# Stores of kept weights, first gates and output transposes: moved in a fused attention, Mish and Sinkhorn-MoE kernel

## The chip, the cores and the metric

One NeuronCore of one Trainium2 chip. The metric is the device time of one execution in microseconds (us). Its engines work side by side, each through its own program in order: TensorE (PE; its weight loads are PEld), VectorE (DVE), ScalarE (ACT), GpSimd (POOL) and SyncE (SP). All DMAs of the part shown here are issued by SP, whose queue also is in order: a DMA that waits for a semaphore holds back those behind it. [...]

## The reference

Three parts in a row, in float32.

- A gated delta-rule attention: 4 batches, 8 heads, 768 positions, head size 48. Keys are normalized, and a 48x48 state per head runs over the positions: `y_t = q_t S`, then `S += beta_t k_t (v_t - k_t S)`.
- A Mish MLP on the 3072 tokens of width 384: `h = x @ w_in` (2048 wide), `g = h * tanh(softplus(h))`, `g @ w_out`.
- A mixture of 8 experts with Sinkhorn gates: `P = exp(logits)` of 3072x8, scaled eight times by row sums and by column sums, then `out = sum over e of P[:, e] * (relu(x @ w1[e]) @ w2[e])`, each expert 1024 wide.

## The kernel before, in words

Each float32 product is made of three products of rounded high and low parts (weights high and low by inputs high, weights high by inputs low), so every operand has a high tile, copied by ACT, and a low tile, a difference made by DVE or POOL.

**First stage.** Six windows (`c` = 0 to 5) of 512 tokens. A window runs 16 Mish units (marks s0 to s15), and then 8 units of expert 0 (marks s16 to s23), each unit with 128 hidden columns. Attention for the next windows is hung on the marks. Weights cycle through six slots (`wslots`): from the second window on each unit's split weights come back from a copy in DRAM by a DMA of 768 KB on SP's queue (line 251, `w<-wd`), issued some three units ahead.

In the last window the second stage is prepared at marks s1 to s15: raw weights of experts 1 to 7 come in (`fetch1` line 432, `fetch2` line 442), ACT and POOL split them (`make1`, `make2`) into three slots `gw`, and `keep` (line 445) stores each split slot to DRAM, `wg`, in two parts of 1280 and 768 KB: units 0 to 2 at marks s5, s6, s9, s10, s13 and s14. While the 8 units of expert 0 run, DVE works off the Sinkhorn rounds, and the gates `P` are final when that stage ends.

**Second stage.** Three units of tokens (`u`, 1024 tokens each), each with 28 steps (7 experts by 4 groups of 256 hidden columns), so 84 steps `s`. A step runs seven groups of first products (line 589, tile `b`, 3 or 6 matmuls each, in the order of `ORDER` = 0, 2, 1, 4, 3, 5, 6; a Strassen-like scheme of seven products). After each group `k` = 0 to 6 come, in this order on the queues: what drains the group into `gt` (DVE line 596, ACT line 598 for the first), the low parts that `late` holds, a weighing of a finished hidden block by its gate and the ReLU (`weigh`: DVE line 622, ACT line 628, low part line 631 on POOL in unit 0 and on DVE after), what `side[k]` holds, five of the 36 second products of the step before (line 652, into six PSUM banks `s`; the last group takes six), and perhaps one `o_store`. First products take their bank from a ring, two banks of `ps_a` as a rule, four in step 0.

In step 0 no second products are there. The weighings wait in `done` until the last group, and each is followed at once by its low part. The gate of expert 1 for the first tokens is spread over partitions in `gate_first`: one DVE multiply of an identity by the gate column (line 547, 128x1024), then two products with a matrix of ones at group 1 (line 555) that ACT copies out (line 556). `gate_out` writes all gates to DRAM: a DVE copy (line 527), two transposes (line 530), an ACT copy (line 532) and two DMAs at group 3; `gate_load` of expert 2 follows at group 4, the others come later, each two steps or more ahead of its use.

At a unit's end the second products of its last step run beside the next unit's first step. After product 26 of 36 half 0 is complete, after product 35 half 1. `o_out` then copies the three banks of a half to `gf` (ACT lines 675 twice, DVE line 673) and puts four stores on `todo`. `o_store` takes one: a bank of the ring, three transposes (line 688), a DVE multiply-add with the gate of expert 0 (line 689) and two output DMAs (line 695). In the loop one store is made after each odd group, so the first one directly behind the copies. Of the last unit no first products are left: its 36 second products run through, with half 0 complete after product 17, and the eight stores follow.

The right side of the on-chip memory is filled from its end: a tile `pad` of 32 bytes a partition, then the weight slots of the first stage and, in the second, `gt`, the high and low hidden tiles, one of the two `gx` tiles and the gates.

Of the kernel before, what the change touches and what calls it, by code (L numbers as in the profile page):

```python
# [8 lines left out]
F32 = mybir.dt.float32  # L9
# [3 lines left out]
AF = mybir.ActivationFunctionType  # L13
# [71 lines left out]
def delta_mish_sinkhorn_kernel(  # L85
# [18 lines left out]
    out_r = out.rearrange("(b s) d -> b s d", b=B)  # L104

    const = ctx.enter_context(tc.tile_pool(name="const", bufs=1))
    ctx.enter_context(tc.tile_pool(name="pad", bufs=1, side="right")).tile([128, 8], F32, name="pad")
    right = ExitStack()
    wpool = right.enter_context(tc.tile_pool(name="wpool", bufs=1, side="right"))
    rawp = ctx.enter_context(tc.tile_pool(name="rawp", bufs=2))  # L110
# [313 lines left out]
        pool2["q"] = ctx.enter_context(tc.tile_pool(name="gq", bufs=1, side="right"))  # L424

    raw1, raw2, wd2 = {}, {}, []

    def fetch1(n):
        if n < UPER:
# [13 lines left out]
            raw2[n] = r  # L443

    def keep(n, lo, hi):
        nc.sync.dma_start(out=wd2[n][:, :, lo:hi], in_=gslots[n % NS2][:, :, lo:hi].bitcast(F32))

    def again(n, lo, hi):
# [75 lines left out]
    def gate_out():  # L524

        q = pool2["q"].tile([128, 3, 192], F32, name="gq")
        nc.vector.tensor_copy(q[:, 0].rearrange("p (e t) -> p e t", e=E), P.rearrange("p t e -> p e t"))
        ps = small[0]()
        for a in range(2):
            nc.tensor.transpose(ps[0:96, a * 128:a * 128 + 128], q[:, 0, a * 96:a * 96 + 96], id_sb)  # L530
        rows = q[0:96, 1:3].rearrange("p a x -> p (a x)")[:, 0:256]
        nc.scalar.activation(out=rows, in_=ps[0:96, 0:256], func=AF.Copy)
        for a in range(2):
            nc.sync.dma_start(out=pe_dram[0][96 * a:96 * a + 96, :], in_=rows[:, 128 * a:128 * a + 128])

    def gate_load(u, e):
        pb = pool2["p"].tile([128, 1024], F32, tag="p", name="gp")
# [6 lines left out]
    def gate_first():  # L544

        a, pb = (pool2["p"].tile([128, 1024], F32, tag="p", name="gp") for _ in range(2))
        nc.vector.tensor_tensor(
            out=a.rearrange("p (t x) -> p t x", x=128), in0=id_sb[:, None, :].to_broadcast([128, 8, 128]),
            in1=P[:, 0:8, 1:2].to_broadcast([128, 8, 128]), op=ALU.mult,
        )  # L550

        def spread_out():
            for i in range(2):
                ps = next_ring("pb")
                mm(ps, lhsT=sk["ones"], rhs=a[:, 512 * i:512 * i + 512], start=True, stop=True)
                nc.scalar.activation(out=pb[:, 512 * i:512 * i + 512], in_=ps, func=AF.Copy)
            pbs[0, 1] = pb

        return spread_out

    ring, ringn = [], [0]

# [94 lines left out]
            seen.add(half)  # L657
        return out

    fin = {}  # L660

    def o_open(u):
        f = pool2[u % 2, "x"].tile([128, 6, 1024], F32, tag="x", name="gf")
# [5 lines left out]
    def o_out(u, half):  # L669
        for d in range(KD):  # L670
            o = fin[u][:, d, 512 * half:512 * half + 512]
            if d == 1:
                nc.vector.tensor_copy(o, os[u][3 * half + d])
            else:
                nc.scalar.activation(out=o, in_=os[u][3 * half + d], func=AF.Copy)
        for t in range(4):
            todo.append((u, half, t))

# [27 lines left out]
    if True:  # L706
# [756 lines left out]
        with tc.manual_schedule():  # L1463
            banks[:] = [0, [A1, A1]]
            for c in range(NBLK):
                pe, rest, late = window(c)
                if c == NBLK - 1:
                    p1.close()
                    open_second()
                    for n in range(2):  # L1470
                        rest["s1"].append(lambda n=n: (fetch1(n), fetch2(n)))
                    rest["s1"].append(lambda: x_fetch(0, 0))
                    for n, f in enumerate((5, 9, 13)):
                        rest[f"s{f}"].append(lambda n=n: all_of(make1(n)))
                        rest[f"s{f + 1}"].append(lambda n=n: all_of(make2(n)))
                    for q, at in enumerate(((3, 4, 7), (11, 12, 15))):
                        for k, f in enumerate(at):
                            if k == 0:
                                rest[f"s{f}"].append(lambda q=q: all_of(x_sums(0, q)))
                            rest[f"s{f}"].append(lambda q=q, k=k: x_split(0, q, k))  # L1480
                    rest["s8"].append(lambda: x_fetch(0, 1))
                m0 = PLACES[0][0]
                b = c * NU

                def side_pe(m, part):
                    return [st() for st in (pe[m][2:] + late[m] if part else pe[m][:2])]

                def side_rest(m, posts):
                    for p in posts:
                        p()  # L1490
                    for r in rest[m]:
                        r()
                    for p in side_pe(m, 1):
                        p()

                rate(0.6)
                for f in range(U1 + 3):
                    m = MARKS[f]
                    posts = side_pe(m, 0)
                    if f < U1:  # L1500
                        ready(b + f)
                        m_first(b + f)
                    if 1 <= f <= U1:
                        m_a(b + f - 1)
                        m_c(b + f - 1)
                    if f == 0 and c:
                        y0_second(b - 1)
                    if f == 1 and c:
                        y0_done(c - 1)
                    if f == 4:  # L1510
                        flush_xr()
                    if f == 2 or not c:
                        banks[1] = [A1, A1, (ps_o1, "o3")]
                    if f == U1 + 1:
                        m_second(b + U1 - 1)
                        x2_done(c)
                    side_rest(m, posts)
                    if 2 <= f <= U1:
                        m_second(b + f - 2)
                    fill(2.0 if c else 1.2)  # L1520
                    if f < U1:
                        if not c:
                            decodes(min(U1, f + 4))
                            converts(min(U1, f + 3))
                            begins(min(U1, f + 5))
                        if ncvt[0] >= U1:
                            conversions(b + f)
                side_rest("f4", side_pe("f4", 0))
                fill(2.0)
                banks[1] = [A1, A1]  # L1530
                last = c == NBLK - 1
                for f in range(U1, NU):
                    u = b + f
                    if last and f > U1 and f % 2 == 0:
                        sink_step()
                    posts = side_pe(f"s{f}", 0)
                    ready(u)
                    if f == U1 + 2:
                        flush_xr()
                    e_first(u, ps_h, mi_p, x1h, x1l)  # L1540
                    if f > U1:
                        e_relu(u - 1)
                    side_rest(f"s{f}", posts)
                    if f > U1:
                        fill(3.6 if c == 0 else 3.2)
                    if last and f > U1 and (f % 2 == 1 or f == U1 + 2):
                        sink_step()
                    if f > U1 + 1:
                        y0_second(u - 2, sink_step if last and f % 2 == 0 and f > U1 + 2 else None)
                    conversions(u)  # L1550
                e_relu(b + NU - 1)
                split = [lambda kc=kc: st_x1(c + 1, kc) for kc in range(KD)] if c + 1 < NBLK else []
                if split:
                    run(*split[0:2])
                y0_second(b + NU - 2)
                if split:
                    run(split[2])
# [9 lines left out]
    with tc.manual_schedule():  # L1567
# [5 lines left out]
        for s in range(N + 1):  # L1573
            ops = seconds(s - 1) if s else []
            if s == N:
                for n, one in enumerate(ops):
                    one()
                    if late and n == 0:
                        late.popleft()()
                while todo:  # L1580
                    o_store()
                break
# [1 line left out]
            k2 = s % UPER  # L1584
            side = {k: [] for k in range(7)}
            if s == 0:
                side[1].append(gate_first())
                side[3].append(gate_out)
                side[4].append(lambda: gate_load(0, 2))
            if s and s + 2 < UPER:  # L1590
                parts = make1(s + 2)
                for k, p in zip((2, 2, 3, 3, 5), parts):
# [27 lines left out]
            for k, a in enumerate(ORDER):  # L1620
                z = drain(s, a, first(s, a))
                while late:
                    late.popleft()()
                if s == 0:
                    done += [z] if z is not None else []
                elif z is not None:
                    late.append(weigh(s, z))
                for p in side[k]:
                    p()
                for one in ops[5 * k:5 * k + 5 if k < 6 else None]:  # L1630
                    one()
                if todo and k % 2 == 1:
                    o_store()
            for z in done:
                late.append(weigh(s, z))
                late.popleft()()
            if s == 0:
                ring[:] = [A1, A1]
                ringn[0] = 0
# [66 lines left out]
```

## Time and profile before

| | us |
|---|---|
| median of 3 runs | 2297.07 |
| the three runs | 2296.84, 2305.61, 2297.07 |
| the profiled execution | 2303.45 |
| its span, first to last instruction | 2301.7 |
| mean granted TensorE clock, share of full speed | 0.971 |

The profile is one execution, and its times are counted from its first instruction. The first stage ends at some 935 us, the second runs to the end. A group of instructions is named by its line, the tile written and the tile read. Of a wait the profile names the releaser that came last.

### The profile page before, as it was taken

The numbers are of one execution on the slowest core, as the hardware profiler recorded it, in microseconds if no ns is written. First come the engines' busy times: TensorE is split into PE (matmuls) and PEld (weight loads), VectorE is DVE, ScalarE is ACT, GpSimd is POOL, SyncE is SP. The second block draws the span as 40 slices with busy tenths as digits, with TensorE's granted clock in tenths as the row PEclk, the third lists the DMA queues.
The fourth block names the chain that finished last, engine by engine and source line by source line (L and its number), as shares of the span: only waits on it lengthen the run. The fifth ranks groups of instructions, "written<-read, shape, count | busy, mean of one in ns | idle before, by whom it ended". The sixth has DMA issues, their size and how long they took to land.

```text
span 2301.7 us, 34912 instructions
## 1 busy us (share of the span) xinstructions
PE 2221.2 (97%) x14262; PEld 1817.4 (79%) x14262; DVE 1356.0 (59%) x2214; ACT 648.2 (28%) x1148; POOL 620.8 (27%) x488
## 2 busy tenths in 40 slices
PE   8788899999999999999999999999999999999998
PEld 6667788788888887788888887888888878888886
DVE  7894726336162134767767766666666666566665
ACT  6453331433323243233333321112112121111111
POOL 4504441432402153376776850000000000000000
PEclk7699999999999999999999999999999999999999
DMA  6385734646354477255555555443443444434342
GB/s 179 128 291 178 238 125 142 183 149 209 128 177 149 162 281 260 75 185 190 195 207 193 190 174 181 151 155 132 157 153 119 176 147 155 139 136 156 124 141 69
DMA packets 121103, 384.25 MB, mean 167 GB/s; under 512 B 9968, under 2 KB 46768, under 8 KB 120944
## 3 DMA queue, kind: packets, MB, share of 16 engines
q1 hardware_dynamic: 120944, 382.03, 48.8%
q8 instruction: 112, 1.84, 0.3%
q14 instruction: 47, 0.39, 0.0%
HBM read 290.14 MB, written 91.85 MB: 166 GB/s over the span
## 4 chain that ended last, share of the span: by engine, by line
PE 87%; DVE 8%; issue 2%; POOL 1%; DMA 1%; ACT 1%; SPq 0%; DVEq 0%; POOLq 0%; ACTq 0%
PE s L652 30%; PE b L589 28%; PE psh L307 11%; PE x L1211 7%; PE y L331 4%; DVE t L993 1%; DVE lane L999 1%; PE psa L930 1%; PE psa L1069 1%; DMA w<-wd 1%; PE psa L1125 1%; PE psa L1230 1%; PE psa L1091 1%; PE psa L1035 1%; DVE lane L963 1%
## 5 line engine op out<-in xcount | busy, mean ns | idle before, releaser
L589 PE MATMUL b<-gx,gw 128*128 128x512 f32 x2772 | 733.9, 393 | 0.1
L596 DVE TENSOR_TENSOR gt<-b,gt 128x512 f32<-128x512 f32 x588 | 398.4, 690 | 423.0 <-PE b L589 412.4
L589 PEld LDWEIGHTS b<-gx,gw 128*128 128x128 f32 x2772 | 519.4, 188 | 116.4 <-DVE gt L596 1.4
L652 PE MATMUL s<-gh,gw 128*128 128x512 f32 x2016 | 575.0, 394 | 1.4 <-ACT gh L628 1.4
L628 ACT ACTIVATE gh<-gt 128x512 fp32r<-128x512 f32 x336 | 212.3, 632 | 968.6 <-DVE gt L622 968.6
L652 PEld LDWEIGHTS s<-gh,gw 128*128 128x128 f32 x2016 | 378.8, 188 | 89.4 <-ACT gh L628 1.8
L307 PE MATMUL psh<-xh,w 128*128 128x512 f32 x864 | 287.8, 415 | 18.9 <-DVE gl L1200 8.4
L652 PE MATMUL s<-gl,gw 128*128 128x512 f32 x1008 | 301.1, 393 | 0.0
L622 DVE SCALAR_TENSOR_TENSOR gt<-gt,gp 128x512 f32<-128x512 f32 x336 | 284.9, 849 | 4.7
L652 PEld LDWEIGHTS s<-gl,gw 128*128 128x128 f32 x1008 | 189.7, 188 | 43.1
L307 PEld LDWEIGHTS psh<-xh,w 128*128 128x128 f32 x864 | 159.6, 194 | 61.8 <-DVE gl L1200 12.4
L1200 POOL TENSOR_TENSOR gl<-x,gh 128x512 fp32r<-128x512 f32 x80 | 103.0, 1288 | 380.6 <-ACT gh L1198 367.5
L631 POOL TENSOR_TENSOR gl<-gt,gh 128x512 fp32r<-128x512 f32 x112 | 165.8, 1488 | 132.5 <-ACT gh L628 70.0
L307 PE MATMUL psh<-xl,w 128*128 128x512 f32 x432 | 175.4, 406 | 0.4 <-DVE xl L786 0.4
L631 DVE TENSOR_TENSOR gl<-gt,gh 128x512 fp32r<-128x512 f32 x224 | 153.2, 684 | 35.2 <-ACT gh L628 35.1
L1211 PE MATMUL x<-gh,w 128*128 128x512 f32 x576 | 153.4, 403 | 0.0
L522 POOL TENSOR_TENSOR gx<-gxr,gx 128x768 fp32r<-128x768 f32 x18 | 33.4, 1858 | 377.9 <-ACT gx L521 376.6
L1211 PEld LDWEIGHTS x<-gh,w 128*128 128x128 f32 x576 | 110.6, 194 | 24.2 <-issue 0.3
L453 POOL TENSOR_TENSOR gw<-gr,gw 128x640 fp32r<-128x640 f32 x56 | 93.3, 1668 | 50.2 <-ACT gw L463 50.2
L307 PEld LDWEIGHTS psh<-xl,w 128*128 128x128 f32 x432 | 84.3, 195 | 21.2 <-DVE xl L786 2.1
L331 PE MATMUL y<-w,hh 128*128 128x384 f32 x384 | 99.3, 339 | 0.0
L1192 ACT ACTIVATE x<-psh 128x512 f32<-128x512 f32 x80 | 47.8, 597 | 144.2 <-PE psh L307 139.8
(196 smaller groups left out, 2271.4 us busy)
## 6 DMA issues: line engine op xcount, KB each, us to landing
w<-wd SPq DMA_DIRECT2D x120, 768.0 KB, 4.4
gw<-wg SPq DMA_DIRECT2D x56, 1280.0 KB, 8.0
gw<-wg SPq DMA_DIRECT2D x56, 768.0 KB, 5.1
wg<-gw SPq DMA_DIRECT2D x28, 1280.0 KB, 6.0
wg<-gw SPq DMA_DIRECT2D x28, 768.0 KB, 5.4
wd<-w SPq DMA_DIRECT2D x24, 768.0 KB, 4.9
gr<-in_w_dram SPq DMA_DIRECT2D x28, 384.0 KB, 3.3
raw<-in_w_dram SPq DMA_DIRECT2D x28, 384.0 KB, 4.0
```

The costliest lines, as they stand in the source:

```text
L307: mm(ps, lhsT=wi(u, pw, kc), rhs=(xh, xl)[px][:, kc, :], start=(n == 0), stop=(n == 3 * KD - 1))
L331: mm(o[t], lhsT=(h, l)[ph][:, t * 128:(t + 1) * 128], rhs=wo(u, pw, 0, DM), start=(f == 0 and n == 0), stop=(f == U2 - 1 and n == 2))
L453: nc.gpsimd.tensor_tensor(out=w[:, 1, lo:hi], in0=r, in1=w[:, 0, lo:hi].bitcast(F32), op=ALU.subtract)
L589: mm(ps, lhsT=w[:, pw, i * 128:i * 128 + 128], rhs=x[:, px, j, :], start=(n == 0), stop=(n == last))
L596: add = lambda o, i: nc.vector.tensor_tensor(out=t[:, o], in0=ps, in1=t[:, i], op=ALU.add)
L622: nc.vector.scalar_tensor_tensor(out=t, in0=t, scalar=0.0, in1=pbs[u, e][:, o:o + 512], op0=ALU.max, op1=ALU.mult)
L628: nc.scalar.activation(out=h, in_=t, func=AF.Copy)
L631: return lambda: eng.tensor_tensor(out=l, in0=t, in1=h.bitcast(F32), op=ALU.subtract)
L652: mm(os[u][3 * half + d], lhsT=w[:, pw, at:at + 128], rhs=hids[s, z][ph], start=(start and new and n == 0), stop=(end and not new and n == 2))
L1192: nc.scalar.activation(out=mi_x[u % 2], in_=hps.pop(u), func=AF.Mish)
L1200: eng.tensor_tensor(out=l, in0=p, in1=h.bitcast(F32), op=ALU.subtract)
L1211: mm(x2ps[c][k], lhsT=wo(u, pw, k * 128, k * 128 + 128), rhs=(h, l)[pg], start=(f == 0 and n == 0), stop=(f == U1 - 1 and n == 2))
```

## The change

The pad grows from 32 to 96 bytes a partition. `keep` puts the stores of units 0 to 2 on a list, and one of the six is issued at each of the marks s17 to s22, beside expert 0. The first gates are made by eight ACT copies of 128x128 with the gate column as scale, and spread in two parts at groups 2 and 3; `gate_out`'s copy goes to ACT, behind group 4, and its transposes, DMAs and the load of expert 2's gate come behind group 6. In step 0 the weighings start at group 4, and their low parts come one group later. A unit's output stores start three groups after a half is complete and then come every second group. In the last products four stores are made between products (after 23, 26, 29 and 32), one at product 35, with three more banks in the ring.

```diff
-    ....tile([128, 8], F32, name="pad")
+    ....tile([128, 24], F32, name="pad")
...
     def keep(n, lo, hi):
+        if n < NS2:
+            kept.append(lambda: store(n, lo, hi))
+        else:
+            store(n, lo, hi)
+
+    def store(n, lo, hi):
         nc.sync.dma_start(out=wd2[n][:, :, lo:hi], in_=gslots[n % NS2][:, :, lo:hi].bitcast(F32))
...
     def gate_out():
-        nc.vector.tensor_copy(q[:, 0].rearrange(...), P.rearrange("p t e -> p e t"))
-        ps = small[0]()
+        nc.scalar.activation(out=q[:, 0].rearrange(...), in_=P.rearrange("p t e -> p e t"), func=AF.Copy)
+        def turn():
+            ps = small[0]()
...
+            gate_load(0, 2)
+        return turn
...
     def gate_first():
-        nc.vector.tensor_tensor(out=a..., in0=id_sb[:, None, :]..., in1=P[:, 0:8, 1:2]..., op=ALU.mult)
-        def spread_out():
-            for i in range(2):
-                ps = next_ring("pb")
-                mm(ps, lhsT=sk["ones"], rhs=a[:, 512 * i:512 * i + 512], start=True, stop=True)
-                nc.scalar.activation(out=pb[:, 512 * i:512 * i + 512], in_=ps, func=AF.Copy)
+        for t in range(8):
+            nc.scalar.activation(out=a[:, 128 * t:128 * t + 128], in_=id_sb, func=AF.Copy, scale=P[:, t, 1:2])
+        def spread_out(i):
+            ps = next_ring("pb")
+            mm(ps, lhsT=sk["ones"], rhs=a[:, 512 * i:512 * i + 512], start=True, stop=True)
+            nc.scalar.activation(out=pb[:, 512 * i:512 * i + 512], in_=ps, func=AF.Copy)
...
     def o_out(u, half):
+        slot[0] = 3
...
+                    for f in range(U1 + 1, NU - 1):
+                        rest[f"s{f}"].append(lambda: kept.popleft()())
...
             if s == N:
+                ring.extend((ps_o1, f"o{k}") for k in range(3))
                 for n, one in enumerate(ops):
                     one()
...
+                    if n > 22 and n % 3 == 2 and todo:
+                        o_store()
...
             if s == 0:
-                side[1].append(gate_first())
-                side[3].append(gate_out)
-                side[4].append(lambda: gate_load(0, 2))
+                spread_out = gate_first()
+                for i in range(2):
+                    side[2 + i].append(spread_out[i])
+                turn = []
+                side[4].append(lambda: turn.append(gate_out()))
+                side[6].append(lambda: turn[0]())
...
-                if s == 0:
-                    done += [z] if z is not None else []
-                elif z is not None:
-                    late.append(weigh(s, z))
+                if z is not None:
+                    done.append(z)
+                if s or k > 3:
+                    for z in done:
+                        late.append(weigh(s, z))
+                    done = []
...
-                if todo and k % 2 == 1:
+                slot[0] -= 1
+                if todo and slot[0] < 0:
                     o_store()
-            for z in done:
-                late.append(weigh(s, z))
-                late.popleft()()
+                    slot[0] = 1
```

## Rows read from the trace of the kernel before

**Rows 1.** The page, part 1: busy time of TensorE, its share, instructions.

```profile
PE 2221.2 (97%) x14262; PEld 1817.4 (79%) x14262; DVE 1356.0 (59%) x2214; ACT 648.2 (28%) x1148; POOL 620.8 (27%) x488
```

**Rows 2.** The page, part 2: clock granted to TensorE in 40 equal slices.

```profile
PEclk7699999999999999999999999999999999999999
```

**Rows 3.** Waits of PE, whole run: us in total, times, longest.

```profile
PE psh L307 <- DMA w<-wd: 5.2, 2, 3.0
PE of L688 <- ACT gf L675: 4.1, 2, 2.1
```

**Rows 4.** Timeline of PE at the end of the kernel.

```profile
2279.56 1.54 PE L652 MATMUL s<-gh,gw 128*128 128x512 f32 x6
2287.80 0.82 PE L688 MATMUL of<-id_sb,gf 128*128 128x128 f32 x6
```

**Rows 5.** Timeline of PE, last mish window: start, us, line, operation, [idle before <-releaser].

```profile
848.56 0.70 PE L307 MATMUL psh<-xh,w 128*128 128x512 f32 x2 [2.96 <-DMA w<-wd]
854.33 0.62 PE L307 MATMUL psh<-xh,w 128*128 128x512 f32 x2
869.01 0.69 PE L307 MATMUL psh<-xh,w 128*128 128x512 f32 x2 [2.28 <-DMA w<-wd]
879.29 0.62 PE L307 MATMUL psh<-xh,w 128*128 128x512 f32 x2
```

**Rows 6.** Stretch around the first stall: busy by engine, PEclk, DMA share, GB/s.

```profile
843.00:856.00 13.00, 10.04 (x38) 7.85 (x37) 0.00 (x0) 3.62 (x5) 4.38 (x4) 0.87 1.02 345
```

**Rows 7.** Chain of waits in the same window: start, us, what.

```profile
839.01 9.42 DMA w<-wd
860.16 8.71 DMA w<-wd
```

**Rows 8.** The page, part 6: issues, KB each, median us to landing.

```profile
w<-wd SPq DMA_DIRECT2D x120, 768.0 KB, 4.4
```

**Rows 9.** Timeline of SP's queue in the same window.

```profile
837.91 0.38 SPq L432 DMA_DIRECT2D gr<-in_w_dram  x1
```

**Rows 10.** DMA traffic from 835 to 870 us: packets, MB, share.

```profile
q1 hardware_dynamic: 3852, 10.23, 83.7%
```

**Rows 11.** DMA traffic from 890 to 935 us, in 40 slices.

```profile
GB/s 418 317 339 421 426 431 419 393 421 421 410 142 38 0 44 257 377 22 0 120 366 213 0 0 0 15 0 0 0 0 0 0 0 0 0 0 0 0 0 0
```

**Rows 12.** Timeline of PE at the first unit's end.

```profile
1389.57 1.54 PE L589 MATMUL b<-gx,gw 128*128 128x512 f32 x6
1394.35 0.82 PE L688 MATMUL of<-id_sb,gf 128*128 128x128 f32 x3 [2.10 <-ACT gf L675]
1399.36 0.85 PE L589 MATMUL b<-gx,gw 128*128 128x512 f32 x3
```

**Rows 13.** Timeline of DVE at the end of the kernel.

```profile
2288.38 2.39 DVE L689 SCALAR_TENSOR_TENSOR gf<-gf,lg,of 128x384 f32<-128x384 f32 x4
```

**Rows 14.** Timeline of SP's queue at the end of the kernel.

```profile
2289.01 10.15 SPq L695 DMA_DIRECT2D out_dram<-gf  x16
```

**Rows 15.** Timeline of PE, first step of the last stage.

```profile
935.22 1.53 PE L589 MATMUL b<-gx,gw 128*128 128x512 f32 x6
942.35 0.39 PE L530 MATMUL sm<-id_sb,gq 128*96 128x128 f32 x2 [1.11 <-DVE gq L527]
948.24 1.44 PE L652 MATMUL s<-gh,gw 128*128 128x512 f32 x5 [1.37 <-ACT gh L628]
951.63 1.66 PE L589 MATMUL b<-gx,gw 128*128 128x512 f32 x6
```

**Rows 16.** Timeline of DVE, first step of the last stage.

```profile
934.27 1.22 DVE L547 TENSOR_TENSOR gp<-id_sb,lg 128x1024 f32<-128x1024 f32 x1
946.84 3.59 DVE L622 SCALAR_TENSOR_TENSOR gt<-gt,gp 128x512 f32<-128x512 f32 x4
```

**Rows 17.** Timeline of ACT, first step of the last stage.

```profile
936.11 0.60 ACT L598 ACTIVATE gt<-b 128x512 f32<-128x512 f32 x1 [0.72 <-PE b L589]
```

**Rows 18.** Groups by line, ACT with a scale operand: busy us, mean ns.

```profile
L885 ACT ACTIVATE vt<-vt,ne 128x48 f32<-128x48 f32 x16 | 3.7, 318 | 0.0
```

More of the change, by code (lines that the diff above doesn't have):

```diff
@@ L106, in delta_mish_sinkhorn_kernel @@
     const = ctx.enter_context(tc.tile_pool(name="const", bufs=1))
-    ctx.enter_context(tc.tile_pool(name="pad", bufs=1, side="right")).tile([128, 8], F32, name="pad")
+    ctx.enter_context(tc.tile_pool(name="pad", bufs=1, side="right")).tile([128, 24], F32, name="pad")
     right = ExitStack()
@@ L426, in delta_mish_sinkhorn_kernel @@
     raw1, raw2, wd2 = {}, {}, []
+    kept = deque()
     def fetch1(n):
@@ L526, in gate_out @@
         q = pool2["q"].tile([128, 3, 192], F32, name="gq")
-        nc.vector.tensor_copy(q[:, 0].rearrange("p (e t) -> p e t", e=E), P.rearrange("p t e -> p e t"))
-        ps = small[0]()
[L529 to L534, printed above, removed]
+        nc.scalar.activation(
+            out=q[:, 0].rearrange("p (e t) -> p e t", e=E), in_=P.rearrange("p t e -> p e t"), func=AF.Copy
+        )
+        def turn():
+            ps = small[0]()
+            for a in range(2):
+                nc.tensor.transpose(ps[0:96, a * 128:a * 128 + 128], q[:, 0, a * 96:a * 96 + 96], id_sb)
+            rows = q[0:96, 1:3].rearrange("p a x -> p (a x)")[:, 0:256]
+            nc.scalar.activation(out=rows, in_=ps[0:96, 0:256], func=AF.Copy)
+            for a in range(2):
+                nc.sync.dma_start(out=pe_dram[0][96 * a:96 * a + 96, :], in_=rows[:, 128 * a:128 * a + 128])
+            gate_load(0, 2)
+        return turn
     def gate_load(u, e):
@@ L546, in gate_first @@
         a, pb = (pool2["p"].tile([128, 1024], F32, tag="p", name="gp") for _ in range(2))
[L547 to L550, printed above, removed]
-        def spread_out():
-            for i in range(2):
-                ps = next_ring("pb")
-                mm(ps, lhsT=sk["ones"], rhs=a[:, 512 * i:512 * i + 512], start=True, stop=True)
-                nc.scalar.activation(out=pb[:, 512 * i:512 * i + 512], in_=ps, func=AF.Copy)
+        for t in range(8):
[4 more added lines that the diff above has]
+            nc.scalar.activation(out=pb[:, 512 * i:512 * i + 512], in_=ps, func=AF.Copy)
             pbs[0, 1] = pb
-        return spread_out
+        return [lambda i=i: spread_out(i) for i in range(2)]
     ring, ringn = [], [0]
@@ L658, in seconds @@
         return out
-    fin = {}
+    fin, slot = {}, [0]
     def o_open(u):
```

## The prediction

> **What bounds the kernel now.** I read the page's busy shares first: TensorE (PE) is busy 97% of the span with 14262 products [rows 1], so a gain has to come out of time in which PE stands still, or runs at the lower clock behind such a stop. The clock row shows 9 tenths or more nearly everywhere after the start [rows 2]. Then PE's waits: where the change works, two stand out, 5.2 us for reloaded weights and 4.1 us for ScalarE's copies at unit ends [rows 3]. Timelines then give the places. Durations come from the profiled execution: span 2301.7, its own time 2303.45, which is 6.4 above the median of 2297.07. A product that nothing holds takes (2287.80 - 2279.56)/36 = 0.229 us [rows 4].
>
> **Stores of the kept weights.** In the last Mish window PE stands twice for a weight load: 2.96 us before 848.56 and 2.28 before 869.01 [rows 5]. Behind each stop products come slowly: 18 from 848.56 take 5.77 where 18 x 0.229 = 4.12, so 1.65 lost; 36 from 869.01 take 10.28 where 8.24, so 2.04 lost. [...] In all 4.61 + 4.32 = 8.9 us.
>
> The loads were issued at 839.01 and 860.16 and took 9.42 and 8.71 to land [rows 7], where the median of all 120 is 4.4 [rows 8]. What lies ahead of each in the DMA queues is a raw-weight load of 384 KB, issued 837.91 [rows 9], and a store of 1280 KB, with one of 768 KB close behind. Two pairs of stores are 4.2 of the 10.2 MB of that stretch [rows 10]. PE wanted the first load at 848.56 - 2.96 = 845.60. Without the store it is issued behind the small load, at 837.91 + 0.38 and a little, 838.4, and has 7.2 us; with only 384 KB before it I estimate 5 (4.4 and part of the small load). The second, issued earlier by the same 0.6, has 866.73 - 859.55 = 7.2 as well. Both stops go: -8.9. The bounds are 0 (the loads still land after 7.2) and -9.4.
>
> Added are six issues at s17 to s22 on SP's queue, beside expert 0. In front of them stand loads that wait for slots, behind them the last reloads, of which each serves a unit three marks later. The DMA engines move little from the 13th of these slices of 1.1 us on, about 904 [rows 11], and the 6.3 MB take some 16 us at the 390 to 430 GB/s of the slices before, with 30 us of room, so I count nothing; if one reload came late as now, it would cost the 4.5 us of one stop. The slots are not rewritten before step 1.
>
> **Unit ends.** At the first, PE waits 2.10 us for ScalarE's copies with the transposes queued ahead of ready products [rows 12]. From 1389.57 to 1399.36 it runs 23 products and three transposes in 9.79. 23 x 0.229 = 5.26, three transposes at most 0.41 (six take 0.82 [rows 4]), so 4.1 is lost, the low clock behind the stop included. The second end is the other 2.0 of the 4.1 us of waits [rows 3]. Three groups later the copies are long done, so the wait goes. What is late next: a store takes one of two PSUM banks, and behind group 4 that makes the next product group wait for a drain of two DVE additions. I charge 0.2 in all, between 0 and 1.2 (a DVE instruction of 0.6 [rows 13] late at each of two places). The later output DMAs shift weight reloads on SP by less than a group, and these have a step of slack. Together -5.9.
>
> **Last products.** After the last product, eight multiply-adds of 2.39/4 = 0.60 feed 16 output DMAs, and SP issues them in 10.15 us, one per 0.634 [rows 13, 14]. From 2289.01 on SP sets the end. After the change the first store starts behind product 23: 2279.56 + 24 x 0.229 = 2285.05, plus 0.58 from transposes to multiply-add [rows 4, 13] and 0.63 from there to the first DMA [rows 13, 14], 2286.26. SP then issues 16 in a row, for a store comes every three products and their transposes (0.69 + 0.41 = 1.10) and SP needs 1.27 for it. The second half is ready at 2287.80 + 4 x 0.41 + 1.21 = 2290.65, before SP is through with the first eight at 2291.3. So the end moves by 2289.01 - 2286.26 = 2.75, and not by half the queue.
>
> [...]
>
> **First step of the last stage.** From 935.22 to 951.63 PE runs 49 products (11.2 us) and six small float32 instructions, estimated at 0.27 each, 1.6; so 3.6 of 16.4 is idle, the most to gain. 1.11 of it waits for the gate copy behind DVE's drains, 1.37 for the first high part behind four weighings that start only at 946.84 and take 3.59 [rows 15, 16]. The DVE multiply of 1.22 [rows 16] goes; it lay under products and gives nothing. The eight ACT copies come before the drain that started at 936.11 [rows 17]. Copies with a scale come 3.7/16 = 0.23 apart at 48 columns [rows 18]; at 128 columns I take 0.30, so 2.4, between 1.85 and 8 x 0.60 = 4.8 [rows 17]. Four banks let PE go on meanwhile until about 938.6, and the drain ends at 938.5: hidden at my value, a stop of 2.4 at the upper end.
>
> Weighings then start near 943, and the first hidden parts are ready before step 1 wants them. Late next are the gate's transposes: their ACT copy stands behind the first two high parts, I estimate until 945.2, where PE arrives at 944.0, 1.25; then step 1's first group waits 0.65 for the bank of group 6, whose drain is behind two weighings on DVE. Idle 1.9 in place of 3.6: -1.7, between -3 and +1. The gates' DMAs come some 5 us later on an empty queue; expert 2 is three steps off.
>
> [...]
>
> **Pad.** The right-side tiles move by 64 bytes. No row shows an address at work; products from right-side hidden tiles are at 0.229 [rows 4]. I take 0. One nanosecond on each of 14262 products would be 14 us either way.
>
> **Sum.** 8.9 + 5.9 + 2.75 + 1.7 = 19.3, so 2303.45 becomes 2284.2 in an execution like the profiled one. The median lies 6.4 below that execution, and its trace can't say where. Low clock makes 1.65 + 2.04 + about 2.0 = 5.7 of my terms. Were the 6.4 all of this kind, the median would fall to 2283.5; were none, to 2277.8. The clock row has its lowest values, 7 and 6, in the first slices [rows 2], so most of it lies elsewhere: 2279.
>
> **Rivals.**
> - *The loads stay late.* SP's load is held until 837.91 by a raw-weight load that itself waits for ScalarE [rows 9], and that stays. If landing needs over 7.2 us without the stores, the Mish term is lost: 2279 + 9 = 2288. For it: 10.2 MB in 35 us there; against: 4.4 for the median load. Chance 0.10.
> - *The spread of the measurement.* Of three runs one took 2305.61, 8.6 above the others, and the profiled one is near it. If two of three runs of the new kernel come out long by that much, the median is 2279 + 8.6 = 2287.6. Against: with fewer stops there is less for the clock to fall behind. Chance 0.13.
> - *More than that.* The upper bounds together (start -3, tail -5, no bank waits), or a pad that helps: 2271. Chance 0.09.
> - *Slower: the pad.* If the new offset lengthens PE's reads or weight loads, it decides from (2297.07 - 2279)/14262 = 1.27 ns a product; at 2.5 ns it adds 36, 2315. Nothing in the rows speaks for it. Chance 0.06, of which 0.05 beyond half a per cent.
>
> **Numbers.** The forecast 2279 has the remaining 0.62, with 2274 to 2285 as its own range. Half a per cent, 11.5 us, is about what a measurement of this kernel can tell from no change, so the bound is 2285.6. Faster 0.62 + 0.09 + 0.04 (the lower parts of the first two rivals) = 0.75; same 0.20; slower 0.05. The range 2270 to 2290 leaves out the pad and the far ends of the others.
>
> **What would show it.** Right: no PE wait for `w` behind 840, weight loads there landing within 7 us, six `wg` stores between 885 and 915; no PE wait at the unit ends; first output DMA of the end near three us earlier relative to the last product, and 16 issues in a row from there; the transposes of the gates as the longest PE wait of step 0. Wrong: products farther apart than 0.229 in undisturbed stretches (the pad); a load for units 20 to 23 that PE waits for; the first drain of step 0 holding PE; a store whose bank holds the next product group for more than 0.6 us.

## The result

The changed kernel takes 2259.70 us (median of four, 2258.78 to 2261.93) beside 2297.99 of the kernel before (2296.84 to 2305.61): 0.983 of it, interval 0.9805 to 0.9851, or 38.3 us less. Forecast were 18.1 less, 2279, with a range that ended at 2270. The direction came true, and the time lies outside the range by more than 10 us. The profiled execution took 2259.81, its span is 2258.0.

The page of the changed kernel (busy us, share, instructions; clock in 40 slices; DMA issues with the median us to landing):

```profile
PE 2191.2 (97%) x14262; PEld 1813.2 (80%) x14262; DVE 1356.8 (60%) x2212; ACT 651.1 (29%) x1157; POOL 622.7 (28%) x488
...
PEclk7698999999999999999999999999999999999999
...
w<-wd SPq DMA_DIRECT2D x120, 768.0 KB, 4.4
```

The clock row is that of [rows 2] but for one slice, and there are as many products as in [rows 1]. PE is busy 30 us less for them. Busy time has no waits in it, so products came closer together; how much of that is less time at a lower granted clock (mean 0.971 before, 0.973 after), the page does not tell. The waits of PE that touch the change (us in total, times, longest):

```profile
PE b L600 <- DVE gt L607: 1.1, 1, 1.1
PE sm L541 <- ACT gq L534: 1.0, 1, 1.0
PE of L700 <- ACT gf L686: 0.2, 1, 0.2
```

The 5.2 us for reloaded weights are gone, and of the 4.1 for the copies at unit ends 0.2 are left, in the tail. Where the time went, by stretches of the two profiled executions (us, between PE instructions; the last Mish window from its first to its last second product, the second stage from its first to its last first product):

| | start | last Mish window | expert 0 | second stage | last second products | to the end | span |
|---|---|---|---|---|---|---|---|
| before | 823.0 | 67.6 | 44.6 | 1342.7 | 9.6 | 14.1 | 2301.7 |
| after | 820.4 | 58.3 | 43.0 | 1315.5 | 10.9 | 10.0 | 2258.0 |
| difference | -2.6 | -9.3 | -1.6 | -27.2 | +1.3 | -4.1 | -43.7 |

The first and the third difference are not the change's: in the profiles of the runs below the start takes 815.8 to 824.5, and expert 0 either 43.0 to 43.1 or 44.5 to 44.7, with and without any of the edits. In the second stage 27.2 went, where the steps of the prediction that lie there, unit ends and first step, make 7.6.

**Last Mish window.** The chain of waits of the changed kernel (start, us, what) is PE alone there, pieces of nine products in 2.04, where [rows 7] have two weight loads:

```profile
836.87 2.04 PE x L1223 x9
838.91 2.04 PE psh L307 x9
...
871.55 2.04 PE psh L307 x9
```

SP's queue in the same window and behind it (start, us, line, operation):

```profile
835.77 0.44 SPq L251 DMA_DIRECT2D w<-wd  x1
...
852.48 0.44 SPq L251 DMA_DIRECT2D w<-wd  x1
...
876.03 0.57 SPq L453 DMA_DIRECT2D wg<-gw  x1
...
897.52 1.18 SPq L453 DMA_DIRECT2D wg<-gw  x2
```

The six stores now lie from 876 to 899, behind most of the reloads (the prediction named 885 to 915), and no reload is waited for afterwards. Reloads issued from 820 to 876 land in 4.5 to 6.7 us, where those of the kernel before, from 820 to 870, took 6.3 to 13.4.

**Unit ends.** PE's timeline at the first:

```profile
1367.13 1.52 PE L600 MATMUL b<-gx,gw 128*128 128x512 f32 x6
...
1372.34 0.84 PE L600 MATMUL b<-gx,gw 128*128 128x512 f32 x3
...
1378.47 0.49 PE L700 MATMUL of<-id_sb,gf 128*128 128x128 f32 x3
```

The 23 products that took 9.79 with three transposes and a wait among them [rows 12] take 5.21, and the transposes come six us behind them without a wait.

**The end.** PE's timeline, and SP's queue in the second fence:

```profile
2244.19 0.49 PE L700 MATMUL of<-id_sb,gf 128*128 128x128 f32 x3
...
2248.67 1.81 PE L700 MATMUL of<-id_sb,gf 128*128 128x128 f32 x12 [0.22 <-ACT gf L686]
```

```profile
2245.36 10.16 SPq L707 DMA_DIRECT2D out_dram<-gf  x16
```

The 16 issues take 10.16 us as before [rows 14], but start 3.3 us ahead of the last twelve transposes.

**First step of the last stage.** PE's timeline:

```profile
921.66 2.92 PE L600 MATMUL b<-gx,gw 128*128 128x512 f32 x12
...
932.08 0.42 PE L541 MATMUL sm<-id_sb,gq 128*96 128x128 f32 x2 [0.96 <-ACT gq L534]
933.60 0.96 PE L600 MATMUL b<-gx,gw 128*128 128x512 f32 x3 [1.09 <-DVE gt L607]
...
937.56 1.52 PE L600 MATMUL b<-gx,gw 128*128 128x512 f32 x6
```

From 921.66 to 937.56 it is 15.90 where [rows 15] have 16.41 for the same 49 products. The last six of the eight gate copies on ACT:

```profile
921.73 1.86 ACT L562 ACTIVATE gp<-id_sb,lg 128x128 f32<-128x128 f32 x6
```

One of them takes 0.39, and the row has six in 1.86, so they start (1.86 - 0.39)/5 = 0.29 apart; 0.30 was assumed. PE did not stand for the drain behind them: its waits in this step are the 0.96 and 1.09 above.

### The profile page after: what moved, and what is told of

Its sections match the earlier page's. It is cut to its first block, busy times and chain, and to the rows that moved or that the text cites. A ratio compares the mean times of both kernels' runs of the same rounds, so it can differ in the third digit from the quotient of the medians.

```text
span 2258.0 us, 34921 instructions
## 1 busy us (share of the span) xinstructions
PE 2191.2 (97%) x14262; PEld 1813.2 (80%) x14262; DVE 1356.8 (60%) x2212; ACT 651.1 (29%) x1157; POOL 622.7 (28%) x488
## 4 chain that ended last, share of the span: by engine, by line
PE 88%; DVE 8%; issue 2%; POOL 1%; ACT 1%; DMA 0%; SPq 0%; DVEq 0%; POOLq 0%; ACTq 0%
PE s L663 30%; PE b L600 28%; PE psh L307 12%; PE x L1223 7%; PE y L331 4%; DVE t L1005 1%; DVE lane L1011 1%; PE psa L942 1%; PE psa L1137 1%; PE psa L1081 1%; PE psa L1242 1%; PE psa L1103 1%; PE psa L1047 1%; DVE lane L975 1%; PE psa L1061 1%
## 5 line engine op out<-in xcount | busy, mean ns | idle before, releaser
L600 PE MATMUL b<-gx,gw 128*128 128x512 f32 x2772 | 726.4, 390 | 1.1 <-DVE gt L607 1.1
L663 PE MATMUL s<-gh,gw 128*128 128x512 f32 x2016 | 565.9, 389 | 0.0
L307 PEld LDWEIGHTS psh<-xh,w 128*128 128x128 f32 x864 | 158.9, 193 | 56.5 <-DVE gl L1212 12.5
L307 PEld LDWEIGHTS psh<-xl,w 128*128 128x128 f32 x432 | 83.1, 192 | 20.9 <-DVE xl L798 2.1
```

The source lines that it names most:

```text
L307: mm(ps, lhsT=wi(u, pw, kc), rhs=(xh, xl)[px][:, kc, :], start=(n == 0), stop=(n == 3 * KD - 1))
L600: mm(ps, lhsT=w[:, pw, i * 128:i * 128 + 128], rhs=x[:, px, j, :], start=(n == 0), stop=(n == last))
L663: mm(os[u][3 * half + d], lhsT=w[:, pw, at:at + 128], rhs=hids[s, z][ph], start=(start and new and n == 0), stop=(end and not new and n == 2))
```

## The experiments

The first theory, from the table: the pad gives the missing 20 us, by the place of the second stage's tiles, and the four other parts give what was forecast for them. The rival: the pad gives nothing, and the later work in the second stage (output stores, gates) removes more waits than were counted. "Pad" stands below for the line `tile([128, 8], F32, name="pad")` of 32 bytes.

**The pad alone, and all but the pad.**

```diff
 # e1, kernel before
-    ... .tile([128, 8], F32, name="pad")
+    ... .tile([128, 24], F32, name="pad")
 # e2, changed kernel
-    ... .tile([128, 24], F32, name="pad")
+    ... .tile([128, 8], F32, name="pad")
```

> Only the pad of before is changed, from 32 to 96 bytes. Theory pad: all of the missing 20 us is here. Second-stage products drop from their 0.229 to 0.232 us to 0.227 each, so 5796 products give 15 to 24 us: about 2276, with the Mish stops, the unit ends and the tail as before. Rival (the other parts were worth double what I summed, the pad nothing): within 4 us of before, spacing unchanged.

> The changed kernel with the old pad of 32 bytes. Theory pad: the other parts give 15 to 20 us, so about 2280, with products back at 0.229 to 0.232 us in the second stage. Rival: 2260 as with the wide pad.

The pad alone: 2278.08 beside 2294.55, 0.9919 (0.9895 to 0.9943). All but the pad: 2282.01, 0.9937 (0.9913 to 0.9960). The two gains are 16.5 and 12.5 us with intervals of some 5 on either side; their sum of 29, some 8 either way, just reaches the 34 to 45 of the whole. In the profiles the second stage of the pad alone takes 1321.0, 21.7 less than before, with every wait of PE still there. So the rival falls. The steps show it directly: one step of unit 1 of the second stage on PE's timeline of the kernel before, the pad alone, and the changed kernel (two like groups, one step of 69 products apart):

```profile
1607.13 0.85 PE L589 MATMUL b<-gx,gw 128*128 128x512 f32 x3
...
1622.92 0.85 PE L589 MATMUL b<-gx,gw 128*128 128x512 f32 x3
```

```profile
1605.41 0.84 PE L589 MATMUL b<-gx,gw 128*128 128x512 f32 x3
...
1621.06 0.84 PE L589 MATMUL b<-gx,gw 128*128 128x512 f32 x3
```

```profile
1603.01 0.84 PE L600 MATMUL b<-gx,gw 128*128 128x512 f32 x3
...
1618.65 0.84 PE L600 MATMUL b<-gx,gw 128*128 128x512 f32 x3
```

15.79, 15.65 and 15.64 us: nothing waits in any of them, and 69 products are 0.15 us shorter. In units 0 and 2 it is 15.93 against 15.64; unit 0 before, and after:

```profile
1196.23 0.85 PE L589 MATMUL b<-gx,gw 128*128 128x512 f32 x3
...
1212.16 0.85 PE L589 MATMUL b<-gx,gw 128*128 128x512 f32 x3
```

```profile
1200.06 0.84 PE L600 MATMUL b<-gx,gw 128*128 128x512 f32 x3
...
1215.70 0.84 PE L600 MATMUL b<-gx,gw 128*128 128x512 f32 x3
```

Over 28 steps of each unit that is 28 x (0.29 + 0.15 + 0.29) = 20.4 us, within the 13 to 24 that the timed runs of the pad alone allow.

**The four other parts, each alone on the kernel before.**

```diff
 # e5: stores of kept weights
+            kept.append(lambda: store(n, lo, hi))     # n < NS2, issued at s17 to s22
 # e6: unit ends
+        slot[0] = 3
-                if todo and k % 2 == 1:
+                slot[0] -= 1
+                if todo and slot[0] < 0:
+                    slot[0] = 1
 # e7: last products
+                ring.extend((ps_o1, f"o{k}") for k in range(3))
+                    if n > 22 and n % 3 == 2 and todo:
+                        o_store()
 # e8: first step: gate_first, gate_out, the weighings from group 4 on
```

> Before with the six stores of kept weights moved beside expert 0, nothing else. Theory (the stops of the last Mish window come from the stores' transfers): no wait of PE for w there, that window 9 us shorter, about 9 us under before. Rival (SP's queue holds the loads): waits of 2 to 3 us stay, gain under 3.

> Before with the output stores three groups later and then every second group, the last products as before. My sum says 5.9 us less: the two waits for the copies of half 0 go (4.1 us) with the slow products behind the first. Rival: the waits turn up at the PSUM ring, under 3 us less.

> Before with four stores between the last products and three more banks. Theory SP (16 issues of 0.63 us in a row set the end): 2.75 us less. [...]

> Before with the first gates on ScalarE and the weighings of step 0 from group 4 on. My sum says 1.7 us less, between 3 less and 1 more: PE waits about 1.25 us for the gate copy and 0.65 for a bank, in place of 1.1 and 1.4 and small ones. [...]

Timed, e5 is 0.9966 (0.9955 to 0.9977) and e6 0.9971 (0.9958 to 0.9984), some 7.8 and 6.7 us; e7 is 0.9991 (0.9976 to 1.0007) and e8 1.0006 (0.9989 to 1.0022), which tell no gain from none. The profiles are finer. The last Mish window of e5 takes 58.3, as in every other profile of a kernel with the later stores, and 65.0 to 68.4 in all that keep the stops; the second stage of e6 takes 1336.4, 6.3 less; the end of e7, from its last first product, 20.9 in place of 23.7.

For e8 the second stage is 2.2 shorter, but not by its edit alone. It has gained 0.67 behind the third group of its second step (0.55 ahead of that group), gains nothing for 27 steps, and then 1.57 at the first unit's end, where it has no edit. The two windows there, before and e8 (us, busy by engine, granted clock, DMA share, GB/s):

```profile
1386.00:1400.00 14.00, 11.86 (x46) 9.12 (x45) 8.85 (x15) 3.39 (x7) 0.00 (x0) 0.88 0.28 103
```

```profile
1383.00:1397.00 14.00, 11.85 (x55) 9.26 (x54) 9.02 (x15) 4.33 (x8) 0.00 (x0) 1.00 0.31 83
```

The wait of 2.10 us is in both, yet only the first has a lower granted clock behind it, 0.88 against 1.00. So the same stop costs 1.6 us more in one execution than in another, and a first step taken at 2.2 would have been a misreading. The two ends of one execution differ as well: in the kernel before, the granted clock is 0.81 from 1391 to 1400, at the first end, and 1.00 from 1840 to 1848, at the second. In the 13 profiles that keep both waits, the lower clock follows 12 of the 26.

**Where the tiles lie.** In the compiled kernel before, the second stage's weights (`gw`, left side) begin 128 bytes above a multiple of 256, and what is streamed from the right side (`gt`, `gh`, `gl`, one `gx`) 192 above one. The larger pad puts the latter at 128 too. Either the absolute place of the right-side tiles decides, or a larger pad does, or the distance of the two operands of a product. The edits:

```diff
 # e3: left side moved by 64, pad as before; e4: the same with the pad of e1
+    ctx.enter_context(tc.tile_pool(name="padl", bufs=1)).tile([128, 16], F32, name="padl")
 # e9, e13, e14, e15, e16: pad alone
+    ... .tile([128, 40], F32, name="pad")    # 72, 56, 16, 32
 # e10: weights moved by 64, what lies behind them on the left (gx too) by 128
+        ctx.enter_context(tc.tile_pool(name="pw", bufs=1)).tile([128, 16], F32, name="pw")   # before gw
+        ctx.enter_context(tc.tile_pool(name="pr", bufs=1)).tile([128, 16], F32, name="pr")   # behind gw
```

> Before with its pad, plus 64 bytes ahead of all tiles on the left side, so left and right tiles start alike, both 64 bytes past a multiple of 128. Theory relative (the weight load reads a left tile while a product streams a right tile, and it counts how the two lie to each other in 128 bytes): products at 0.227 us, about 2276. Theory absolute (a right-side operand must start at a multiple of 128): no gain, about 2298.

> Before with both: left tiles start 64 bytes past a multiple of 128, right tiles at a multiple. Theory relative: slow products, 0.229 to 0.232 us, about 2298. Theory absolute: products at 0.227, at least those with right-side operands, 2276 to 2285.

> Before with a pad of 160 bytes: the right tiles lie 128 bytes from where before has them. Theory (only the place within 128 bytes counts): products at 0.229 to 0.232 us as in before, time within 4 us of it. Rival (any larger pad helps, or the place within 256 bytes or more): products at 0.227, about 20 us less.

> Before with 64 bytes ahead of the second stage's weight slots on the left and 64 behind them, so the weights alone move: 64 past a multiple of 128, like the right-side tiles, while the left gx tile of units 0 and 2 stays at a multiple. Theory (weight load against streamed operand): unit 1, where every streamed operand is on the right, runs at 0.227 instead of 0.229; in units 0 and 2 first products are now the ones that disagree, and stay slow, 0.229 to 0.232 on average. Rival (the streamed operand's own place counts): unit 1 stays at 0.229.

> Before with a pad of 288 bytes, 256 more. Let the offset be the place of the streamed right tile less that of the left weights, modulo 256: before +64, the 160-byte pad -64. Theory period 256: as before, unit 1 at 0.2289 us a product, the time within 4 us. Rival (longer period): another spacing.

> Before with a pad of 224 bytes: offset 128 of 256. Theory 128-byte rows (only being off a row start together counts): 0.2267 us, about 20 us less than before. Theory 256: slower than at 0, between 0.2267 and 0.2333.

> Before with a pad of 64 bytes: offset +32 of 256. If the price grows with the offset: unit 1 between 0.2267 and 0.2289 us. If any offset costs the same: 0.2289.

> Before with a pad of 128 bytes: offset -32 of 256. If the price grows with the offset and is dearer on this side: unit 1 between 0.2267 and 0.2333 us. If any offset on this side costs the same: 0.2333, some 12 us above before.

Unit 1 streams right-side tiles only, so it has one distance (streamed operand minus weights, modulo 256 bytes). The table sorts by it; spacing is the mean from product to product in unit 1, steps are of 69 products.

| kernel | distance | spacing, ns | step of units 0, 1, 2, us | time / before (interval) |
|---|---|---|---|---|
| after | 0 | 226.7 | 15.64, 15.64, 15.64 | |
| e1, pad 24 | 0 | 226.7 | 15.64, 15.64, 15.64 | 0.9919 (0.9895 to 0.9943) |
| e3, left side +64 | 0 | 226.7 | 15.64, 15.64, 15.64 | 0.9903 (0.9881 to 0.9925) |
| e10, weights +64 | 0, unit 1 only | 226.7 | 15.95, 15.64, 15.95 | 0.9981 (0.9962 to 1.0001) |
| before | +64 | 228.9 | 15.93, 15.79, 15.93 | |
| e2, all but the pad | +64 | 228.9 | 15.93, 15.79, 15.93 | 0.9937 (0.9913 to 0.9960) |
| e13, pad 72 | -192, as +64 | 228.9 | 15.93, 15.79, 15.93 | 1.0000 (0.9979 to 1.0021) |
| e14, pad 56 | 128 | 232.4 | 15.93, 16.03, 15.93 | 1.0033 (1.0015 to 1.0050) |
| e15, pad 16 | +32 | 233.3 | 16.03, 16.10, 16.03 | 1.0068 (1.0032 to 1.0104) |
| e16, pad 32 | -32 | 233.3 | 15.94, 16.10, 15.94 | 1.0044 (1.0028 to 1.0060) |
| e9, pad 40 | -64 | 233.3 | 16.00, 16.10, 16.00 | 1.0049 (1.0030 to 1.0067) |
| e4, left +64, pad 24 | -64 | 233.3 | 16.00, 16.10, 16.00 | 1.0068 (1.0043 to 1.0093) |

The step of unit 1 in e9, at a distance of -64, on PE's timeline:

```profile
1604.49 0.86 PE L589 MATMUL b<-gx,gw 128*128 128x512 f32 x3
...
1620.59 0.86 PE L589 MATMUL b<-gx,gw 128*128 128x512 f32 x3
```

And in e10, where of all that unit 1 reads the weights alone moved, by 64 bytes:

```profile
1606.43 0.84 PE L591 MATMUL b<-gx,gw 128*128 128x512 f32 x3
...
1622.07 0.84 PE L591 MATMUL b<-gx,gw 128*128 128x512 f32 x3
```

16.10 and 15.64. What follows:

- A larger pad is no help as such: e9 and e14 have a larger pad than e1 and are slower than before. Nor does the place of the right-side tiles decide: e3 leaves them where they were and gains all of it, e4 gives them the place of e1 and loses. In the first stage weights and streamed tiles lie on the right side together and move with the pad together, and there the spacing is 0.2267 us in before, e9, e14, e15 and e16 alike, at five different places in 256 bytes.
- Of what unit 1 reads, e10 moves nothing but the weights, by 64, and brings that unit, whose streamed operands are all from the right side, to 15.64. So weights and streamed operand count against one another. Units 0 and 2 stay slow: their first products stream a `gx` from the left side, which e10 moves by 128 and so from distance 0 to +64.
- Of the distances tried only 0 is fast. e13, 256 bytes away from the distance before, repeats its steps to 0.01 us, so the pattern has a period of 256 bytes as far as two such places can show it; a period of 128 falls, for 128 is not as 0 (e14, 232.4 ns against 226.7).
- The price does not grow with the distance: +32 and -64, at 233.3 ns, are dearer than +64, at 228.9.
- A product's own distance does not set its own pace. In unit 0 of the kernel before the first products, at distance 0, come 229.9 ns apart and the second products with the high part (`gh`), at +64, 233.6; in e10, where it is the other way round, 230.9 and 232.8. The table's 226.7 holds where all products of a stretch are at distance 0.

Several expectations missed. A period of 128 bytes, the theory of e9 and one of the two of e14, failed, as did the rival in e9 that a larger pad helps. e15 came out at 233.3, above both values named for it, and e4 was dearer than the 0.229 to 0.232 expected. Those of e3, e10, e13 and, with its dearer value, e16 held.

Why the distance counts is not settled. A clash of PE's two reads, weights of the next product and rows of this one, would fit, for weight loads lie beside the products (79% and 97% of the span [rows 1]), but it is the author's guess: no run looks at the reads themselves. Open is also why units 0 and 2 of the kernel before lose twice what unit 1 loses (0.29 us a step against 0.15), though their first products, 33 of the 69 of a step, read the left `gx`, at distance 0.

**The changed kernel again, and with two queues for the last output.**

```diff
 # e12, changed kernel, each second output DMA of the last unit
-    nc.sync.dma_start(...)
+    (nc.scalar if u == NU2 - 1 and q else nc.sync).dma_start(...)
```

> The changed kernel beside the runs before and behind it: about 37 us under before, 2260.

> The changed kernel with every second output DMA of the last unit issued by ScalarE's queue instead of SP's. Theory SP (the queue's 16 issues set the end): the eight issues left on SP take 5 us from 2245, so the end is set by the last product's stores instead, about 2 to 3 us under the changed kernel. Rival (transfers or landings set the end): no difference.

e11 took 2263.20, 0.9845 of before (0.9807 to 0.9882), and e12 2258.76, 0.9822 (0.9793 to 0.9851): all four times of e12 lie below those of e11, but the intervals overlap and two of the four lie within the first times of the changed kernel, so it is not shown to be faster. In its profile the end behind the last product falls from 10.0 to 8.6, less than the 2 to 3 us expected. SP's queue and ACT's in e12:

```profile
2245.62 8.16 SPq L707 DMA_DIRECT2D out_dram<-gf  x8
```

```profile
2245.62 3.57 ACTq L707 DMA_DIRECT2D out_dram<-gf  x4
2249.24 1.08 ACT L686 ACTIVATE gf<-s 128x512 f32<-128x512 f32 x2 [5.26 <-DMA out_dram<-gf]
2251.39 2.69 ACTq L707 DMA_DIRECT2D out_dram<-gf  x4
```

Eight issues on SP still span 8.16 us, for ACT's copies of the second half stand behind its own first four issues. By these rows the limit is now the order on ACT and no longer SP's queue; no run moved those copies.

## Why the prediction was wrong

The step that failed is the pad: "No row shows an address at work; products from right-side hidden tiles are at 0.229. I take 0." It measured 20.4 us by the steps (16.5 in the timed runs of the pad alone): in the second stage the weights and what is streamed beside them lay 64 bytes apart modulo 256, and the larger pad brings them to 0. The forecast was a fall of 18.1, and 18.1 + 20.4 = 38.5 beside the 38.3 measured. Agreement that close is in part luck: the timed gains of e1 and e2 add up to 29, and a part of what the unit ends and the stops gave goes by the execution. But no other term is off by more than some 1 us.

The trace of the kernel before did hold the sign. Its chain of waits in the first stage, ahead of the stops, where weights and streamed tiles are on the same side:

```profile
831.32 2.04 PE x L1211 x9
833.36 2.04 PE psh L307 x9
```

A product takes 2.04/9 = 0.2267 there, in the same shape, at a granted clock of 1.00 (831 to 836) and without a wait, and 0.229 to 0.231 in the second stage. The prediction took the 0.229 of [rows 4] as the pace of "a product that nothing holds" and asked only whether the pad could disturb it. The question was the other one: what holds the second stage at 0.229 already. The pace is not a matter of how late the stage comes: with e1 and e3 the second stage runs at 0.2267 to its end. The rival "a pad that helps" was there, at 0.09 and with no more than 8 us for all its parts; the rival "slower: the pad", with 1.27 ns a product as its point, was the same mechanism with the other sign, and a pad of 40 or 16 columns in place of 24 is that case (e9, e15).

The others, as predicted and as the profiles show them (us):

| step | predicted | measured | from |
|---|---|---|---|
| stores of the kept weights | -8.9 | -9.3 | last Mish window, before to after and to e5 |
| unit ends | -5.9 | -6.3 | second stage of e6 |
| last products | -2.75 | -2.9 (-2.8 in e7) | last first product to the end |
| first step | -1.7 | -0.7 | e8 behind the third group of its second step |
| pad | 0 | -20.4 | steps of units 0 to 2 |

- *Stores.* Both stops went, and no late reload came in their place. The rival that the loads stay late is out: PE never waits for them here. With its stops that window took 65.0 to 68.4, so they cost 6.7 to 10.1 by the execution; the prediction's 8.9 was read from one of the dearer ones.
- *Unit ends.* As worked out. In 5.21 us for 23 products nothing is lost. Some 1.6 of the 6.3 is the lower clock behind the first stop (0.81 from 1391 to 1400), which 14 of the 26 such stops do not have; against an execution without it the same edit would have shown some 4.7.
- *Last products.* The end is set by SP's 16 issues in a row, 10.16 us of them (10.15 before), as the sum has it. Half the queue, 10.15/2 = 5.1 us, which is the tail in the prediction's upper bounds together, did not go: the profiles show 2.9 and, in e7, 2.8, while the timed e7, some 2 us less with 3.5 either way, cannot tell 2.8 from 5.1. Even two queues (e12) gave 1.4.
- *First step.* The two waits that were said to come next came, 0.96 and 1.09 where 1.25 and 0.65 were estimated. Mis-sized is the idle time before: the six small float32 instructions were put at 0.27 each, an estimate; in the kernel before the two transposes have 0.28 and the four products with ones 0.59. In e8 the 15.86 us of that stretch less 2.05 of waits and 49 x 0.229 leave 2.6 us for them, not 1.6, and so 2.6 of the 16.4 were idle and not 3.6.
- *From execution to median.* 5.2 us of low clock and scatter were taken off for the profiled execution. Where the prediction counts 1.65, 2.04 and some 2.0 of low clock, the trace of before has a granted clock of 0.70 (848.56 to 854.33), 0.83 (869.01 to 879.29) and 0.81 (1391 to 1400). The two profiled executions differ by 43.6 and the medians by 38.3, so 5.3 was about right. It was not in the stops alone: the start and expert 0, where no edit shows, make 4.2 of it.

## What to carry to other kernels

Compare the spacing of equal products between the stages of a kernel before taking any of them as undisturbed: two stages at 0.2267 and 0.229 us with no wait in either are a loss with a place, here 20 us of 2300. Where one is slower, move one tile by 32 to 128 bytes at a time and look at the step period, which shows 0.1 us in 16. Price a change of offsets by its best and worst neighbour, not by nothing; and take the cost of a stop from several executions, since the lower clock behind it came in some and not in others (behind 12 stops of 26 here).

## What was not expected of the hardware

- The spacing of 128x128 by 128x512 products of this kernel depends on where the two operands lie against one another: where all products of a stretch have one distance, 226.7 ns at equal places modulo 256 bytes, 228.9 at +64, 232.4 at 128, 233.3 at +32, -32 and -64.
- The same wait of 2.10 us at a unit's end was followed by a granted clock of 0.88 over 14 us in one execution and of 1.00 in another, a difference of 1.6 us.
